# A recurrence and mixer kernel: first loads cast on the way, six masks on other engines, three sums ahead of the fourth

## The chip, the cores and the metric

One core of a Trainium2 chip. The metric is the device time of one execution in microseconds (us), and the smaller the better. Engines are named as in the profile: PE does matmuls and transposes, DVE, ACT and POOL work on elements, SP and POOL issue transfers. Unless a ratio is given, times are medians of runs of one kernel.

## The reference, cut to what matters

Four batches, eight heads, 768 steps of 64 elements. A decaying recurrence over q, k and v gives x; a token mixing and then a channel mixing follow.

```python
for t in range(S):                                    # per head, decay gamma
    state = gamma * state + outer(k[t], v[t])
    y[t]  = scale * q[t] @ state
x  = y as (batch, 768, 512)
u  = x + (relu(x^T @ w_tok1) @ w_tok2)^T              # token mixing, 768 -> 256 -> 768
out = u + relu(u @ w_ch1) @ w_ch2                     # channel mixing, 512 -> 1536 -> 512
```

The kernel does two heads (a "pair") at a time, in blocks of 128 steps. "ch1" and "ch2" are the two matmuls of the channel mixing. For batch 0 a half of ch1 is 12 groups of four matmuls, one for each pair, 48 in all. "All ch1" below means this first half.

## The kernel before

Every instruction is described as an `Op` with an engine, a priority, an assumed duration and what it depends on. A list scheduler, `arrange()`, then puts them into one order for each engine. So the order on PE is fixed when the kernel is built, by assumed times; on the chip PE follows it and waits where an input is late.

```python
        # front(b, p): loads of pair p of batch b, all through SP, all as float32
        for nm, src in (("k", k), ("q", q), ("v", v)):
            def emit(nm=nm, src=src):
                t = tile_of(sl[nm], sb, [P, 2 * NC, D], FP)
                ...
                    dma = nc.sync.dma_start(out=t, in_=rows.rearrange("h (c p) d -> p (h c) d", p=P))
                if b == 1:
                    tc.add_manual_dep(dma.ins, wops["c1", 1].ins.ins.name, ...,
                        reason="the weights come first")
        ...
        kc = op(KENG, 900, 980, emit, [ld["k"]], [K], [sl["k"]])       # k scaled, to f16, on DVE
        qc = op("POOL", 770, 830, cast(Q, sl["q"]), [ld["q"]], [Q], [sl["q"]])
        vc = op("POOL", 770, 830, cast(V, sl["v"]), [ld["v"]], [V], [sl["v"]])
        ...
        def turn(src, dst, dep, eng):        # six transposes on PE, then a copy out of PSUM
            ...
            t = op("PE", 340, 500, emit, [dep, ...], [T], [src])
        ...
        pp = op("PE", 300, 470, emit, [kc, vc, ...], [ST], [K, V])      # the first sum step, k^T v
        ...
                def emit(hf=hf, j=j, A=A):                              # the mask, 16 of them a batch
                    nc.vector.tensor_tensor(am, src[:, :HC], mask, ALU.mult)
        ...
        FA = "ba" if first else "fa"         # batch 0's token mixing: three PSUM buffers "ba"

    # back(b): the channel mixing
                for half_cts in (cts[:NP // 2], cts[NP // 2:]):
                    c1 = op("PE", 328, 490, lambda e=emit, q=half_cts: e(q),
                            [uT_done[b, p, sh] for p in range(NP)] + [wops["c1", ...], c1], ...)

    # at the end: zero matmuls ("fillers") where the schedule expects PE to wait at the start
                idle[0] = max(0, int((o.start - end - 40) / (220 if end > 1500 else 500)))
```

A "turn" is what the text calls the six transposes that bring k or q of a pair into the other layout.

Of the kernel before, what the change touches and what calls it, by code (L numbers as in the profile page):

```python
# [17 lines left out]
def kernel(  # L18
# [56 lines left out]
    make_identity(nc, ident16)  # L75

    gp = const_p.tile([P, NP], FP, name="gp")
    for p in range(NP):
# [4 lines left out]
    nc.gpsimd.affine_select(  # L83
        out=mask, in_=mask, compare_op=ALU.is_ge, fill=0.0,
        base=0, pattern=[[0, HC], [1, P]], channel_multiplier=-1,
    )
# [12 lines left out]
    BUFS = dict(kf=4, qf=4, vf=4, k16=3, q16=3, v16=4, kT=4, qT=4, U=3, am=8, x16=2, h1=4, u16=3, u16w=2,  # L99
# [3 lines left out]
    LONG, XK, XQ, XU, XBAR, RING = 2, 2, 2, 2, 1500, 3  # L103
# [18 lines left out]
    def arrange():  # L122


        way = {}
        for op in reversed(ops):
            if op.first is not None:
                way[op] = way.get(op, 0) + op.lat + SEM
                for d in op.deps:
                    way[d] = max(way.get(d, 0), way[op])  # L130
        for op in ops:
            if op.first is not None:
                op.prio = (op.prio[0], 0, EARLY * op.first - way[op], op.first)
        free = dict(PE=5000, ACT=5000, DVE=4600, POOL=4000, SP=1300, DMA=1300)
        taken = {t: [] for t in BUFS}
        todo, order, ring = list(ops), [], []
        while todo:
            best = []
            for op in todo:
                if any(d.end is None for d in op.deps):  # L140
                    continue
                start = free[op.eng]
                if op.dma and op.eng == "SP" and len(ring) >= RING:
                    start = max(start, ring[-RING])
                for d in op.deps:
                    if d.eng == op.eng and (d.dma or d.eng == "PE"):
                        continue
                    start = max(start, d.end + (30 if d.eng == op.eng else SEM) + op.guard)
                more = {}
                for s in op.takes:  # L150
                    q = taken[s.tag]
                    n = len(q) + more.get(s.tag, 0) - BUFS[s.tag]
                    more[s.tag] = more.get(s.tag, 0) + 1
                    if n >= 0:
                        old = q[n]
                        if any(u.end is None for u in old.users):
                            break
                        start = max([start] + [u.end + SEM for u in old.users])
                else:
                    best.append((start, op))  # L160
            t = min(b[0] for b in best)

            eng = min(best, key=lambda b: (b[0], b[1].prio))[1].eng
            start, op = min((b for b in best if b[1].eng == eng and b[0] <= t + 20),
                            key=lambda b: b[1].prio)
            free[op.eng] = start + op.occ
            op.start = start
            if op.dma:
                free["DMA"] = max(free["DMA"], start + 50) + op.dma
                op.end = free["DMA"] + 1600  # L170
                if op.eng == "SP":
                    ring.append(free["DMA"])
            else:
                op.end = start + op.lat
            for s in op.takes:
                taken[s.tag].append(s)
            todo.remove(op)
            order.append(op)
        return order
# [16 lines left out]
    def weight(key, ns, out, src, dep):  # L196
        def emit():
            return nc.gpsimd.dma_start(out=out, in_=src.rearrange("(i p) j -> p i j", p=P))
        wops[key] = Op("POOL", (0,) if key in ("t1", "t2", ("c1", 0)) else (1, 0, 99), 800, 800, emit, deps=[dep], dma=ns)


    load_done = [None]
# [4 lines left out]
    def front(b, p):  # L207
# [20 lines left out]
        sl, ld = {}, {}  # L228
        for nm, src in (("k", k), ("q", q), ("v", v)):
            sl[nm] = Slot(nm + "f")  # L230

            def emit(nm=nm, src=src):
                t = tile_of(sl[nm], sb, [P, 2 * NC, D], FP)
                rows = src[b, 2 * p:2 * p + 2]
                if nm == "q" and b < LONG:

                    dma = nc.sync.dma_start(  # L237
                        out=t.rearrange("p (h f i) d -> p h f (i d)", h=2, f=2),
                        in_=rows.rearrange("h (f p i) d -> p h f (i d)", f=2, p=P))
                else:  # L240
                    dma = nc.sync.dma_start(out=t, in_=rows.rearrange("h (c p) d -> p (h c) d", p=P))  # L241
                if b == 1:
# [4 lines left out]
            ld[nm] = Op("SP", (0, b, p), 100, 100, emit,  # L247
                        deps=[load_done[-1]] + ([wops["c1", 1]] if b == 1 else []),
                        takes=[sl[nm]], dma=1200 if nm == "q" and b < LONG else 1750)
            load_done.append(ld[nm])  # L250

        K, Q, V = Slot("k16"), Slot("q16"), Slot("v16")

        def emit():
            k16 = tile_of(K, sb, [P, NC, 2, D], F16)
            for j in range(2):
                h = 2 * p + j
                src = sl["k"].tile[:, j * NC:(j + 1) * NC, :]
                if KENG == "ACT":
                    nc.scalar.mul(k16[:, :, j, :], src, gk[:, h:h + 1])  # L260
                else:
                    nc.vector.tensor_scalar(k16[:, :, j, :], src, gk[:, h:h + 1], None, ALU.mult)  # L262
        KENG = "DVE"
        kc = op(KENG, 900, 980, emit, [ld["k"]], [K], [sl["k"]])

        def cast(slot, src):
            def emit():
                t = tile_of(slot, sb, [P, NC, 2, D], F16)
                nc.gpsimd.tensor_copy(t.rearrange("p c h d -> p h c d"),  # L269
                                      src.tile.rearrange("p (h c) d -> p h c d", h=2))  # L270
            return emit
        qc = op("POOL", 770, 830, cast(Q, sl["q"]), [ld["q"]], [Q], [sl["q"]])
        vc = op("POOL", 770, 830, cast(V, sl["v"]), [ld["v"]], [V], [sl["v"]])
        KT, QT = Slot("kT"), Slot("qT")

        def turn(src, dst, dep, eng):
            T = Slot("fa")

            def emit():
                T.tile = tp = tile_of(T, ps, [P, 512], FP).bitcast(F16)  # L280
                for c in range(NC):
                    nc.tensor.transpose(tp[:, c * P:(c + 1) * P],  # L282
                                        src.tile[:, c].rearrange("p h d -> p (h d)"), ident16)
# [11 lines left out]
        def crossbar(src, dst, dep):  # L295
            def emit():
# [3 lines left out]
                    in_=src.tile.rearrange("p c h d -> p (c h d)"))  # L300
# [7 lines left out]
        def emit():  # L308
            st = tile_of(ST, ps, [P, 512], FP)
            for c in range(NC - 1):  # L310
                for j in range(2):
                    nc.tensor.matmul(st[j * D:(j + 1) * D, c * D:(c + 1) * D], K.tile[:, c, j],  # L312
                                     V.tile[:, c, j], start=True, stop=True)
# [20 lines left out]
        def emit():  # L334
            nc.vector.tensor_scalar(RS.tile[D:, :, D:], US.tile[D:], g128[2 * p + 1], None, ALU.mult)
        r1 = op("DVE", 400, 480, emit, [prev, r0], [], [US, RS])
# [4 lines left out]
        for hf in range(2):  # L341
# [12 lines left out]
            for j in range(2):  # L354
                def emit(hf=hf, j=j, A=A):
                    am = tile_of(AM[2 * hf + j], sb, [P, HC, P], F16)
                    src = A[j].tile.rearrange("p (i t) -> p i t", t=P)
                    nc.vector.tensor_tensor(am, src[:, :HC], mask, ALU.mult)  # L358
                am_ops.append(op("DVE", 470, 550, emit, [a], [AM[2 * hf + j]], [A[j]]))
        X16 = Slot("x16")  # L360
        x_ops, xf = [], []
        for hf in range(2):
            Y = Slot("fa")

            def emit(hf=hf, Y=Y):
                y = tile_of(Y, ps, [P, 512], FP)
                R = RS.tile
                for i in range(HC):
# [5 lines left out]
                    for j in range(2):  # L374
                        nc.tensor.matmul(o[:, j * D:(j + 1) * D], AM[2 * hf + j].tile[:, i],  # L375
                                         V.tile[:, c, j], start=(c == 0), stop=(c == 0 or j == 1))
# [42 lines left out]
        FA = "ba" if first else "fa"  # L419
# [8 lines left out]
        t1 = op("PE", 690, 860, emit, x_ops + [wops["t1"], None if first else t2_done.get(b * NP + p - 1)], [T1], [X16])  # L428
# [10 lines left out]
        for hf in range(2):  # L439
# [9 lines left out]
            t2 = op("PE", 350, 520, emit, [hr, wops["t2"]], [T2], [H1])  # L449
# [64 lines left out]
    def back(b):  # L514
# [6 lines left out]
        for sh in range(2):  # L521
            H2 = Slot("h2")
            rel = []
            for ft in range(NF):
# [12 lines left out]
                for half_cts in (cts[:NP // 2], cts[NP // 2:]):  # L537
                    c1 = op("PE", 328, 490, lambda e=emit, q=half_cts: e(q),
                            [uT_done[b, p, sh] for p in range(NP)] + [wops["c1", int(ft >= CUT1[0][1])], c1],
# [8 lines left out]
            for i in range(HC):  # L548
# [3 lines left out]
                for part in range(parts):  # L552
# [25 lines left out]
                    op("SP", 100, 100, emit, [ad], [], [O]).dma = 800 // parts  # L578


    weight("t1", 2000, wt1, moe_w_tok1, None)
    weight("t2", 2000, wt2, moe_w_tok2, None)
    for i, (f0, f1) in enumerate(CUT1):
        weight(("c1", i), 650 * (f1 - f0), wc1[i], moe_w_ch1[:, f0 * P:f1 * P], None)
    weight(("c2", 0), 7800, wc2, moe_w_ch2, None)
    casts = [front(0, p) for p in range(NP)]
    after = {"t1": casts[2][2], ("c1", 0): casts[3][1]}
    last = None
    for key, o in wops.items():
        o.deps += [d for d in (after.get(key), last) if d is not None]  # L590
        last = o

    for b in range(1, B):
        for p in range(NP):
            front(b, p)
    for b in range(B):
        back(b)
    end, mixing = 1500, False
    for o in arrange():
        if o.eng == "PE":  # L600
            mixing = mixing or o.prio[0] == 1
            if o.takes and not mixing:

                idle[0] = max(0, int((o.start - end - 40) / (220 if end > 1500 else 500)))
# [32 lines left out]
```

## Time and profile before

| | before |
|---|---|
| time | 208.95 us (208.68 to 209.27, 3 runs) |
| span of the profiled run (208.47 us), clock | 206.8 us, 1.00 |
| last v of batch 0 landed, usable | 22.54 us, 24.40 us |
| first ch1 matmul | 37.91 us |
| batch 1's first k issued, landed | 34.56 us, 44.21 us |
| all ch1 and both turns of batch 1's first pair (counted) | 46.56 us |

The span runs from the first to the last instruction; the time is some 1.7 us longer. The clock is the mean share of full TensorE speed that the core was granted. The page gives PE's share and the two transfer queues; in the queue lines the numbers are packets, megabytes and a share of the 16 engines' span.

```profile
PE 198.9 (96%) x1898; PEld 120.5 (58%) x1898; DVE 114.8 (56%) x291; ACT 96.2 (47%) x205; POOL 61.9 (30%) x107
...
q1 hardware_dynamic: 89104, 29.89, 72.6%
q0 software_dynamic: 3664, 3.93, 11.4%
```

PE at 96% reads like a PE-bound kernel. It is one from 38 us on; before that its row holds fillers (62 records). A line of the timeline has the columns: start, us, engine, line, operation, output and inputs, shape, count, and in brackets the idle time before it and what ended it.

```profile
108.43 0.23 PE L372 MATMUL fa<-r,qT 128*128 128x128 f16 x1 [0.31 <-DVE r L335]
```

It is PE's only idle time over 0.1 us between 40 us and the tail.

### The profile page before, as it was taken

The numbers are of one execution on the slowest core, as the hardware profiler recorded it, in microseconds if no ns is written. First come the engines' busy times: TensorE is split into PE (matmuls) and PEld (weight loads), VectorE is DVE, ScalarE is ACT, GpSimd is POOL, SyncE is SP. The second block draws the span as 40 slices with busy tenths as digits, with TensorE's granted clock in tenths as the row PEclk, the third lists the DMA queues.
The fourth block names the chain that finished last, engine by engine and source line by source line (L and its number), as shares of the span: only waits on it lengthen the run. The fifth ranks groups of instructions, "written<-read, shape, count | busy, mean of one in ns | idle before, by whom it ended". The sixth has DMA issues, their size and how long they took to land.

```text
span 206.8 us, 4738 instructions
## 1 busy us (share of the span) xinstructions
PE 198.9 (96%) x1898; PEld 120.5 (58%) x1898; DVE 114.8 (56%) x291; ACT 96.2 (47%) x205; POOL 61.9 (30%) x107
## 2 busy tenths in 40 slices
PE   6899899999999999999999999999999999999993
PEld 2554487564667667576656574458556545545552
DVE  6377896114998878996794726686663021021021
ACT  7237458674497842455502670176215604604600
POOL 2338852113345635252533134115311000000000
PEclk9999999999999999999999999999999999999999
DMA  6999999999999999989995899996722012012012
GB/s 165 248 244 247 188 207 201 202 263 237 295 271 213 189 203 230 226 177 162 212 171 141 145 216 218 155 263 107 152 101 75 17 51 101 3 51 101 0 54 101
DMA packets 92790, 34.13 MB, mean 165 GB/s; under 512 B 81888, under 2 KB 89312, under 8 KB 92768
## 3 DMA queue, kind: packets, MB, share of 16 engines
q1 hardware_dynamic: 89104, 29.89, 72.6%
q0 software_dynamic: 3664, 3.93, 11.4%
q8 instruction: 15, 0.25, 0.5%
q14 instruction: 7, 0.06, 0.1%
HBM read 26.74 MB, written 6.29 MB: 160 GB/s over the span
## 4 chain that ended last, share of the span: by engine, by line
PE 83%; SPq 5%; DMA 4%; DVE 3%; ACT 2%; issue 1%; POOL 0%; DVEq 0%
PE ba L532 31%; PE ba L561 29%; PE fa L426 4%; DMA kf<-in_k_dram 4%; PE fa L447 4%; PE fa L351 3%; SPq L241 3%; PE fa L375 3%; SPq L237 2%; PE fa L372 2%; PE fa L282 2%; PE fa L312 2%; DVE k L262 1%; PE ba L426 1%; PE ba L189 1%
## 5 line engine op out<-in xcount | busy, mean ns | idle before, releaser
L532 PE MATMUL ba<-uT,wc 128*128 128x384 f16 x384 | 68.4, 326 | 0.0
L561 PE MATMUL ba<-wc,h 128*128 128x512 f16 (+1 forms) x300 | 67.7, 371 | 0.0
L545 ACT ACTIVATE h<-ba 128x384 f16<-128x384 f32 x96 | 46.7, 490 | 41.3 <-PE ba L532 40.4
L532 PEld LDWEIGHTS <-wc 128*128 128x128 f16 x384 | 35.5, 98 | 22.2
L570 DVE TENSOR_TENSOR o<-x,ba 128x512 f32<-128x512 f32 (+1 forms) x25 | 16.6, 663 | 50.1 <-PE ba L561 49.7
L561 PEld LDWEIGHTS <-h 128*128 128x128 f16 x300 | 27.6, 98 | 27.0
L358 DVE TENSOR_TENSOR am<-fa,mask 128x384 f16<-128x384 f32 x64 | 32.7, 550 | 5.3 <-PE fa L351 4.8
L403 POOL CAST x<-x 128x384 f16<-128x384 f32 x30 | 15.0, 512 | 37.6 <-issue 20.4
L269 POOL CAST q<-qf 128x768 f16<-128x768 f32 x16 | 13.7, 854 | 29.3 <-DMA qf<-in_q_dram 24.7
L386 ACT ACTIVATE x<-fa,gy 128x192 f32<-128x192 f32 (+1 forms) x42 | 15.1, 417 | 9.2 <-PE fa L375 8.7
L262 DVE TENSOR_SCALAR k<-kf,gk 128x384 f16<-128x384 f32 x32 | 14.5, 495 | 7.6 <-DMA kf<-in_k_dram 7.5
L189 PE MATMUL fa<-zero 128*128 128x512 f16 x54 | 15.9, 425 | 2.4 <-DVE zero L52 1.3
L331 ACT ACTIVATE r<-U 64x320 f16<-64x320 f32 x16 | 7.4, 465 | 23.2 <-DVE U L324 23.2
L324 DVE SCALAR_TENSOR_TENSOR U<-U,gp,fa 128x64 f32<-128x64 f32 x64 | 17.1, 275 | 1.0
L454 DVE TENSOR_TENSOR x<-x,fa 128x384 f32<-128x384 f32 x24 | 12.5, 549 | 6.3 <-POOL q L269 3.1
L291 ACT COPY qT<-fa 128x768 f16<-128x768 f16 x8 | 11.6, 1455 | 6.5 <-PE fa L282 6.5
L269 POOL CAST v<-vf 128x768 f16<-128x768 f32 x16 | 13.2, 827 | 4.6 <-DMA vf<-in_v_dram 3.7
L375 PE MATMUL fa<-v,am 128*128 128x64 f16 x192 | 13.9, 193 | 0.0
L375 PEld LDWEIGHTS <-am 128*128 128x128 f16 x192 | 12.1, 98 | 1.9
L426 PEld LDWEIGHTS <-wt 128*128 128x128 f16 x192 | 11.7, 98 | 2.6 <-issue 0.4
L447 PEld LDWEIGHTS <-wt 128*128 128x128 f16 x192 | 11.8, 98 | 2.0
L465 POOL CAST u16w<-x 128x384 f16<-128x384 f32 x16 | 7.9, 506 | 14.7 <-DVE x L454 14.6
(53 smaller groups left out, 164.3 us busy)
## 6 DMA issues: line engine op xcount, KB each, us to landing
kf<-in_k_dram SPq DMA_DIRECT2D x16, 384.0 KB, 6.5
qf<-in_q_dram SPq DMA_DIRECT2D x16, 384.0 KB, 6.1
vf<-in_v_dram SPq DMA_DIRECT2D x16, 384.0 KB, 5.8
out_dram<-o SPq DMA_DIRECT2D x23, 256.0 KB, 2.3
wc<-in_moe_w_ch_dram POOLq DMA_DIRECT2D x1, 1536.0 KB, 18.9
wc<-in_moe_w_ch_dram POOLq DMA_DIRECT2D x1, 1024.0 KB, 11.7
wt<-in_moe_w_tok_dram POOLq DMA_DIRECT2D x2, 384.0 KB, 6.9
wc<-in_moe_w_ch_dram POOLq DMA_DIRECT2D x1, 512.0 KB, 7.3
```

The costliest lines, as they stand in the source:

```text
L189: nc.tensor.matmul(slot.tile, zero[:, :P], zero, start=True, stop=True)
L262: nc.vector.tensor_scalar(k16[:, :, j, :], src, gk[:, h:h + 1], None, ALU.mult)
L269: nc.gpsimd.tensor_copy(t.rearrange("p c h d -> p h c d"), src.tile.rearrange("p (h c) d -> p h c d", h=2))
L324: nc.vector.scalar_tensor_tensor(U[:, c], U[:, c - 1], gp[:, p:p + 1], o, ALU.mult, ALU.add)
L358: nc.vector.tensor_tensor(am, src[:, :HC], mask, ALU.mult)
L375: nc.tensor.matmul(o[:, j * D:(j + 1) * D], AM[2 * hf + j].tile[:, i], V.tile[:, c, j], start=(c == 0), stop=(c == 0 or j == 1))
L426: nc.tensor.matmul(acc[:, jt * P:(jt + 1) * P], wt1[:, i, jt * P:(jt + 1) * P], X16.tile[:, i], start=(i == 0), stop=(i == NC - 1))
L447: nc.tensor.matmul(acc[:, i * P:(i + 1) * P], wt2[:, jt, t], H1.tile[:, jt], start=(jt == 0), stop=(jt == NJ - 1))
L532: nc.tensor.matmul(acc[:, :SH], w[:, ct, f * P:(f + 1) * P], UT.tile[:, ct, sh * SH:(sh + 1) * SH], start=(ct == 0), stop=(ct == NP - 1))
L545: nc.scalar.activation(H2.tile[:, ft], A.tile[:, :SH], AF.Relu)
L561: nc.tensor.matmul(A.tile[:, :CW], H2.tile[:, ft, i * P:(i + 1) * P], wc2[:, ft, cs], start=(ft == 0), stop=(ft == NF - 1))
L570: nc.vector.tensor_tensor(o[:, :CW], X.tile[:, sh * HC + i, cs], A.tile[:, :CW], ALU.add)
```

## The change

The intent: bring batch 0 in sooner and start ch1 sooner. q and v of batch 0 are cast to f16 by the transfer itself, which puts them on POOL's queue; k of pairs 1 to 3 goes there too. Six of batch 0's sixteen masks are made by an ACT copy and a POOL select. The ch1 sums of the first three pairs may go ahead of the fourth. The estimate behind the fillers is cut by a quarter. The diff also moves the token mixing of pairs 2 and 3 from the three buffers "ba" to the five called "fa". The core of it:

```diff
-    LONG, XK, XQ, XU, XBAR, RING = 2, 2, 2, 2, 1500, 3
+    RING = dict(SP=3, POOL=8)
+    ASIDE, RACT = ((1, 1), (1, 3), (2, 1), (2, 3), (3, 1), (3, 3)), ()
+    FILL, TOKBA = 0.75, 2
 ...
+                eng = nc.gpsimd if first and p else nc.sync
 ...
+        def cast(slot, nm):
+            if first:
+                def emit():
+                    t = tile_of(slot, sb, [P, 2 * NC, D], F16)
+                    ...
+                    return nc.gpsimd.dma_start(out=t, in_=rows.rearrange("h (c p) d -> p (h c) d", p=P))
+                o = Op("POOL", (0,), 1000, 1000, emit, [], [slot], dma=QLONG if nm == "q" else 1400)
+                queue.append(o)
+                return o
 ...
+                    if src is Q and first:
+                        for j in range(2):
+                            nc.tensor.transpose(tp[j * D:(j + 1) * D, c * P:(c + 1) * P],
+                                                src.tile[:, j * NC + c], ident16)
+                        continue
 ...
+                    if off:
+                        nc.scalar.copy(am, src[:, :HC])
+                    else:
+                        nc.vector.tensor_tensor(am, src[:, :HC], mask, ALU.mult)
+                if off:
+                    def emit(M=M):
+                        nc.gpsimd.affine_select(out=M.tile, in_=M.tile, compare_op=ALU.is_ge, ...)
 ...
-        FA = "ba" if first else "fa"
+        FA = "ba" if first and p < TOKBA else "fa"
 ...
-                for half_cts in (cts[:NP // 2], cts[NP // 2:]):
-                    c1 = op("PE", 328, 490, lambda e=emit, q=half_cts: e(q),
-                            [uT_done[b, p, sh] for p in range(NP)] + ...
+                for some in (cts[:NP - 1], cts[NP - 1:]):
+                    c1 = op("PE", 164 * len(some), 164 * len(some) + 160, lambda e=emit, q=some: e(q),
+                            [uT_done[b, p, sh] for p in some] + ...
 ...
-                idle[0] = max(0, int((o.start - end - 40) / (220 if end > 1500 else 500)))
+                idle[0] = max(0, int((o.start - end - 40) * FILL / 220 if end > 1500 else (o.start - end) / 450))
```

(Cut: the scheduler's new model of two queues, the order of POOL's issues, the identity and the mask made later.)

## The prediction

> **What bounds the kernel now.** I read the page's forty slices first, then the sums by stretch, the chain that ended last, the timeline of the first 56 us, and the trace's landing and packet records behind it.
>
> The slices show two regimes.
>
> ```profile
> PE   6899899999999999999999999999999999999993
> DVE  6377896114998878996794726686663021021021
> PEclk9999999999999999999999999999999999999999
> DMA  6999999999999999989995899996722012012012
> ```
>
> A slice is 5.17 us. PE looks busy from the second slice on, but until about 38 us part of that is filler: L189 multiplies zeros and holds 15.9 us. DMA is at 9 from the second slice to the nineteenth. The stretches and the chain say when PE becomes the true bound:
>
> ```profile
> 20.00:25.00 5.00, 4.21 (x46) 1.91 (x42) 4.05 (x13) 3.02 (x6) 3.72 (x5) 1.00 1.29 198
> 25.00:30.00 5.00, 4.95 (x92) 4.24 (x89) 4.60 (x13) 2.62 (x8) 2.82 (x6) 1.00 1.16 198
> ...
> 60.00:80.00 20.00, 20.00 (x263) 14.14 (x262) 16.90 (x40) 12.44 (x28) 9.84 (x17) 1.00 1.14 209
> 80.00:120.00 40.00, 39.69 (x443) 25.27 (x442) 30.56 (x76) 17.42 (x41) 14.50 (x26) 1.00 1.02 180
> 120.00:160.00 40.00, 40.00 (x381) 24.07 (x378) 23.31 (x52) 14.99 (x36) 12.81 (x22) 1.00 0.86 160
> ```
>
> ```profile
> 12.24 7.61 DMA kf<-in_k_dram
> ...
> 38.08 7.80 PE ba L532 x48
> ```
>
> The columns of the first are stretch, length, then busy us of PE, PEld, DVE, ACT, POOL, clock, DMA share, GB/s. From 38 us PE has some 0.3 us of idle time until the tail. So the 168.8 us from there to the end (206.8 - 38.0) are PE work in one row, and this change leaves that work alone. Only two things can move the time: when the first ch1 matmul starts, and whether PE waits after that.
>
> The first 38 us are paced by DMA. By the landing records the twelve loads of batch 0 land from 4.52 us (first k) to 22.54 us (last v), each k or v about 1.75 us behind the one before it, each q about 1.25. Then, without a gap, land wt1 24.65, wt2 26.52, the first ch1 weights 29.30, the rest of ch1 34.49, ch2 43.27. Batch 1's loads may only be issued when the ch1 weights are in, and run beside ch2's:
>
> ```profile
> 34.56 0.37 SPq L241 DMA_DIRECT2D kf<-in_k_dram  x1
> ...
> 37.91 7.96 PE L532 MATMUL ba<-uT,wc 128*128 128x384 f16 x48
> ...
> 44.23 0.75 DVE L262 TENSOR_SCALAR k<-kf,gk 128x384 f16<-128x384 f32 x2 [7.20 <-DMA kf<-in_k_dram]
> ...
> 45.53 0.83 POOL L269 CAST q<-qf 128x768 f16<-128x768 f32 x1 [7.86 <-DMA qf<-in_q_dram]
> ...
> 46.15 0.50 PE L282 MATMUL fa<-ident,k 128*128 128x128 f16 x6
> ```
>
> The reader is to see that batch 1's first k was issued at 34.56 and landed only at 44.21, after ch2. DVE and POOL sat idle for it, PE did not: its first use of that k, the turn at 46.15, stands behind all 48 ch1 matmuls. That slack is 1.2 us.
>
> **What the Trainium skill says.** "DMA: Bandwidth & Descriptors", section "SWDGE vs HWDGE vs iDMA": a DMA that casts must be issued from GpSimd. The trace agrees as far as it goes: the weights, the only casting loads, are on q0, software_dynamic, 3664 packets. Its section "Issuing engines are not separate DMA queues" says that all issuers share the same 16 DMA engines; so a second queue adds no bandwidth, and I count bytes and packets, not queues. Its section "Queues, rings and completion order" says that each engine goes round-robin between its queues by packet. The packet records agree: from 39 to 41 us, q0 (ch2) started 155 and 150 packets in the two microseconds and q1 (k) 148 and 159, though a ch2 packet reads eight times the bytes; and kf's first packets came only at 38.0, 3.5 us after the issue. "TensorE: Matmul & The Clock Gate", Part 1, says that an idle window of about 3.4 us drops the clock; the trace has no such gap and a clock of 1.00 everywhere.
>
> **The change, part by part.**
>
> *Cast loads for batch 0.* q and v come as f16 through POOL's queue; k of pairs 1 to 3 joins them; only the first k is left on SP. Removed: eight POOL casts of 0.83 us (6.6 us of POOL), which stood between a landing and its use. The last v is usable at its landing instead of 24.40 (cast start 23.56 + 0.84). Added: eleven issues on POOL. The weights' issues took 0.70 to 1.03 us each, so about 10 us, done well ahead of the data. What a casting packet costs I fit on the weights' landings: wt1, 48 packets per engine of 1024 B source, 2.11 us, 44 ns each; the second ch1 piece, 32 of 4096 B, 5.19 us, 162 ns. A line through both is 4.7 ns + 0.0384 ns per byte (wt2's 3072 B: 122 against 117 measured). Estimates from it: v, 96 packets of 256 B, 14.5 ns each, 1.4 us; q, 32 of 768 B, 34 ns, 1.1 us. With k at 1.75 a pair costs 4.25 us, four 17.0. From the first packets at 2.0 us, with 0.5 us to land, that is 19.5 for the last v; I take 20.0, because k through the software queue was never seen and the small packets are extrapolated. So inputs and every weight behind them come about **2.5 us** earlier.
>
> *Six masks by ACT and POOL.* Six of sixteen DVE masks at 0.55 us go: 3.3 us off DVE, which is 4.6 of 5 busy from 25 to 30 us. Each becomes an ACT copy (about 0.47) and a POOL select (0.52 for the same size, L83 at start), longer in latency but beside other work. Worth perhaps 0.5 to 1 us in the last pair's chain.
>
> *First ch1 sums.* The ordering of instructions shows what it comes to: three ch1 matmuls, one group's three pairs, ahead of the last transpose. 3 x 0.163 = 0.5 us.
>
> *Fillers.* L189's issues go from about 60 to 40; they stand in waits, and the removal gains at most tenths where one overran. The q turn has twelve half-width matmuls instead of six: 4 x 0.34 = 1.3 us of PE at worst, while PE waits anyway.
>
> Sum up to the first ch1 matmul: before, 13.5 us from usable v (24.40) to 37.91. After, 20.0 + about 13 = **33 us**, some 5 us earlier, if nothing else binds.
>
> **But most of this should be lost again.** The new PE order puts batch 1's k turn after 35 of the 48 ch1 matmuls, not behind all 48, and PE is in order. PE would reach it at 33 + 35 x 0.163 = 38.7. That k still has to wait for the ch1 weights and to share with ch2; both move by only the 2.5 us: landing 44.2 - 2.5 = 41.7, scaled by DVE (0.75 and a start) at 42.5. PE idles almost 4 us. Then turn 0.34, 12 ch1 1.96, q turn 0.34, last ch1 0.16: at 45.3 all ch1 and both turns are done. Before, the same work (ch1 done 45.88, plus two turns of 0.34) counts to 46.56. Gain **1.25 us**, or in general the DMA's gain less 1.25. Later turns have slack: the second k lands near 46.2 and is wanted near 51. From there PE is the bound again.
>
> **Rivals.**
> 1. *The start binds, not the load*: if batch 1's k comes in time, the whole gain at the first ch1 stays, 4 to 5 us, 204 to 205 us. For: POOL and DVE are relieved, and someone chose this order. Against: kf's 9.65 us from issue to landing beside ch2, which the change does not touch.
> 2. *Small casting packets are dear*: their recorded durations extrapolate to 34 ns for v's 256 B against 24 for k's on SP. If throughput followed that, a pair would cost 1 us or more extra, and inputs come 3 us later: 212 to 214 us. Against: packets overlap, and landings fit the line above.
> 3. *POOL becomes the bound*: issues, six selects and sixteen casts stand in one in-order row, and the first x cast is caught between weight issues. It could cost 1 to 2 us at the start; as the wait for k has almost 4 us of room, little of it would show: 207 to 209 us.
> 4. *The clock drops in the 4 us wait*: then some us of matmuls run slow, up to 2 us lost, 209 to 210 us. It would need a whole quiet window.
>
> **Range and chances.** The middle case is 208.95 - 1.25 = 207.7; I lean slightly to the fast side for rival 1 and for k packets that may be cheaper in the software queue (if like v's, three times 0.35 us): 207.3 us. An input gain of 0.5 to 4 us gives 209.7 to 206.2; with some room for rival 1, 205.0 to 209.3. Faster by over 2% (under 204.8) needs rival 1 nearly in full: 0.16. Slower by over 2% (over 213.1) needs rival 2 in full: 0.03.
>
> **What would show it.** Right: last v landing near 20 and ch2 near 41; first ch1 matmul between 32 and 35 us; PE idle for 3 to 4 us before the k turn of batch 1, released by DVE, itself released by kf; from about 46 us on, PE's row as before. Wrong: no such idle time (rival 1); last v landing after 22 (rival 2); the first ch1 matmul after 37 with POOL as releaser (rival 3); a clock below 1.00 (rival 4); or new idle time of PE after 60 us, which I have counted as nil.

## The result, and the profile after

206.81 us (205.84 to 207.07, 4 runs) against 209.08 us of before in the same session: ratio 0.9893, 95% interval 0.9857 to 0.9929. A ratio here is the mean time of one kernel's fast runs over the mean of the other's in the same rounds, so not quite the ratio of the medians quoted. The profiled run took 205.84 us, span 204.1 us, clock 1.00.

| | before | predicted | after |
|---|---|---|---|
| last v landed | 22.54 | 20.0 | 19.70 |
| ch2's weights landed | 43.27 | 41 | 40.75 |
| first ch1 matmul | 37.91 | 33 | 33.66 |
| batch 1's first k landed | 44.21 | 41.7 | 41.66 |
| PE idle before that k's turn | 0 | almost 4 | 2.81 |
| all ch1 and both turns | 46.56 | 45.3 | 45.45 |
| last ch2 matmul issued | 202.95 | | 200.63 |

The slices of the changed kernel (5.10 us each), and the lines that answer to those of before on the page:

```profile
PE   6598999769999999999999999999999999999993
...
DMA  7999999989799999999997999898531112012012
...
q1 hardware_dynamic: 76128, 25.57, 61.3%
q0 software_dynamic: 12320, 6.69, 23.2%
```

PE's ninth slice, 40.8 to 45.9 us, is a 6, where the two slices ahead of it are 9 and 7. Batch 0's inputs have moved from q1 to q0. Sums by stretch make the hole sharper (length; busy us of PE, PEld, DVE, ACT, POOL; clock; DMA share; GB/s):

```profile
40.00:42.00 2.00, 0.00 (x0) 0.00 (x0) 0.32 (x1) 0.00 (x0) 0.00 (x0) 1.00 1.10 232
42.00:44.00 2.00, 1.51 (x14) 1.06 (x15) 0.43 (x2) 0.96 (x2) 0.83 (x1) 1.00 0.96 214
```

From 40 to 42 us PE does nothing at all, and the transfer engines are as busy as ever. The timeline says what it waits for:

```profile
31.45 0.38 SPq L256 DMA_DIRECT2D kf<-in_k_dram  x1
...
33.66 0.65 PE L597 MATMUL ba<-uT,wc 128*128 128x384 f16 x3
...
34.31 5.36 PE L597 MATMUL ba<-uT,wc 128*128 128x384 f16 x32
...
41.68 0.75 DVE L313 TENSOR_SCALAR k<-kf,gk 128x384 f16<-128x384 f32 x2 [8.46 <-DMA kf<-in_k_dram]
...
42.49 0.51 PE L332 MATMUL fa<-ident,k 128*128 128x128 f16 x6 [2.81 <-DVE k L313]
...
42.84 2.11 PE L597 MATMUL ba<-uT,wc 128*128 128x384 f16 x12
```

The reader is to see the order on PE: 35 ch1 matmuls, then the turn of batch 1's k, then the last 13. The turn stands where the schedule expected k to be in. It came at 41.66 us, DVE scaled it in 0.75 us, and 13 matmuls that had all they needed stood behind it.

Where the 2.63 us between the two profiled spans lie: 1.1 us up to 45 us (the table's sixth row); 0.3 us after the last ch2 matmul; and 1.2 us in between, which I had counted as nil. Start-to-start times of PE's instructions give most of that 1.2: the idle 0.31 us at 108.43 is gone, and 0.8 us lie in the ch1 matmuls. They step at 0.16 us, but 0.26 us where one of the matmuls of half the rows or columns (the scores, the sum step) follows; after 45 us there are 12 such steps before and 4 after. Nobody put them there: the schedule fell out otherwise.

### The profile page after: what moved, and what is told of

The parts are those of the page before. It is cut to its first block, busy times and chain, and to the rows that moved or that the text cites. A ratio compares the mean times of both kernels' runs of the same rounds, so it can differ in the third digit from the quotient of the medians.

```text
span 204.1 us, 4737 instructions
## 1 busy us (share of the span) xinstructions
PE 192.3 (94%) x1900; PEld 118.8 (58%) x1900; DVE 112.6 (55%) x285; ACT 97.4 (48%) x211; POOL 69.2 (34%) x116
## 4 chain that ended last, share of the span: by engine, by line
PE 81%; DMA 8%; DVE 6%; ACT 2%; issue 1%; POOL 0%; POOLq 0%; DVEq 0%
PE ba L626 31%; PE ba L597 28%; DMA kf<-in_k_dram 5%; PE fa L491 5%; PE fa L512 4%; PE fa L403 4%; DMA v<-in_v_dram 3%; PE fa L440 2%; DVE k L313 2%; PE fa L437 2%; PE fa L361 2%; DVE am L416 1%; PE fa L332 1%; ACT qT L340 1%; DVE U L373 1%
## 5 line engine op out<-in xcount | busy, mean ns | idle before, releaser
L626 PE MATMUL ba<-wc,h 128*128 128x512 f16 (+1 forms) x300 | 68.9, 371 | 0.0
L610 ACT ACTIVATE h<-ba 128x384 f16<-128x384 f32 x96 | 46.4, 492 | 39.2 <-PE ba L597 38.7
L597 PEld LDWEIGHTS <-wc 128*128 128x128 f16 x384 | 36.0, 98 | 22.5
L416 DVE TENSOR_TENSOR am<-fa,mask 128x384 f16<-128x384 f32 x58 | 29.9, 551 | 11.8 <-PE fa L403 11.7
L519 DVE TENSOR_TENSOR x<-x,fa 128x384 f32<-128x384 f32 x28 | 14.5, 551 | 11.6 <-PE fa L512 11.2
L313 DVE TENSOR_SCALAR k<-kf,gk 128x384 f16<-128x384 f32 x32 | 15.8, 534 | 8.5 <-DMA kf<-in_k_dram 8.5
L292 POOL CAST q<-qf 128x768 f16<-128x768 f32 x12 | 10.2, 849 | 21.4 <-DMA qf<-in_q_dram 20.5
L292 POOL CAST v<-vf 128x768 f16<-128x768 f32 x12 | 9.9, 827 | 8.6 <-DMA vf<-in_v_dram 7.9
L194 PE MATMUL fa<-zero 128*128 128x512 f16 x37 | 10.7, 423 | 2.2 <-DVE zero L52 1.3
L340 ACT COPY qT<-fa 128x768 f16<-128x768 f16 x8 | 11.5, 1443 | 2.1 <-PE fa L328 1.7
```

The costliest lines, as they stand in the source:

```text
L292: nc.gpsimd.tensor_copy(t, src.tile.rearrange("p (h c) d -> p h c d", h=2))
L313: (nc.gpsimd if keng == "POOL" else nc.vector).tensor_scalar(k16[:, :, j, :], src, gk[:, h:h + 1], None, ALU.mult)
L597: nc.tensor.matmul(acc[:, :SH], w[:, ct, f * P:(f + 1) * P], UT.tile[:, ct, sh * SH:(sh + 1) * SH], start=(ct == 0), stop=(ct == NP - 1))
L610: nc.scalar.activation(H2.tile[:, ft], A.tile[:, :SH], AF.Relu)
L626: nc.tensor.matmul(A.tile[:, :CW], H2.tile[:, ft, i * P:(i + 1) * P], wc2[:, ft, cs], start=(ft == 0), stop=(ft == NF - 1))
```

## The experiments

Twelve kernels. The runs of one batch share their runs of the kernel before: 208.65 us for the first four, 209.0 for the next four, 208.86 for the last four. Theory: PE's place for batch 1's first turn is what throws away the earlier start, because the k behind it is tied to the weights. Rivals: the six masks or the fillers are what counts; the clock falls in the wait; or the loads alone do it.

| run | what it is | time, us | ratio to before (95%) |
|---|---|---|---|
| e1 | both turns held behind ch2's first matmuls | 203.49 | 0.9748 (0.9730 to 0.9767) |
| e2 | 12 fillers in the wait | 205.76 | 0.9877 (0.9846 to 0.9908) |
| e3 | batch 1's first k ahead of ch2's weights | 203.92 | 0.9768 (0.9748 to 0.9788) |
| e4 | masks on DVE | 207.81 | 0.9948 (0.9917 to 0.9979) |
| e5 | the changed kernel again | 207.15 | 0.9900 (0.9865 to 0.9934) |
| e6 | loads of batch 0 as before | 213.96 | 1.0241 (1.0210 to 1.0272) |
| e7 | the cast loads alone | 208.95 | 0.9996 (0.9975 to 1.0017) |
| e8 | ch1 in halves, after all four pairs | 207.06 | 0.9917 (0.9879 to 0.9954) |
| e9 | e1, and the first sum step held | 205.32 | 0.9845 (0.9815 to 0.9875) |
| e10 | e9 with masks on DVE | 203.71 | 0.9753 (0.9735 to 0.9771) |
| e11 | e9 with loads of batch 0 as before | 208.16 | 0.9970 (0.9953 to 0.9986) |
| e12 | e9 with all token mixing in "ba" | 204.68 | 0.9798 (0.9780 to 0.9815) |

### e1: the turns held back

```diff
             t = op("PE", 340, 500, emit, [dep, ...], [T], [src])
+            if (b, p) == (1, 0):
+                late.append(t)
 ...
     for b in range(B):
         back(b)
+    late[0].deps.append(ch2[1])      # k turn not before the 4th ch2 matmul
+    late[1].deps.append(ch2[4])      # q turn not before the 10th
```

> The changed kernel with one ordering rule added: batch 1's first k turn not before the fourth ch2 matmul, its q turn not before the tenth. No DMA is touched. My theory (the new order puts the k turn 2.8 us before its data): the idle 2.81 us of PE before the k turn goes, k still lands near 41.7 us, ch2's weights near 40.7; span 204.1 - 2.8 = 201.3, time about 203 to 204, ratio to before 0.971 to 0.976, clock 1.00 in all runs. Rival (DMA bounds that stretch whatever the order): the wait only moves to ch2's weights, v or the second pair, and the time stays at 206 to 207.

203.49 us. The timeline:

```profile
33.30 7.48 PE L600 MATMUL ba<-uT,wc 128*128 128x384 f16 x45
...
40.62 1.03 PE L629 MATMUL ba<-wc,h 128*128 128x512 f16 x4
40.81 0.75 DVE L314 TENSOR_SCALAR k<-kf,gk 128x384 f16<-128x384 f32 x2 [8.60 <-DMA kf<-in_k_dram]
...
41.62 0.51 PE L333 MATMUL fa<-ident,k 128*128 128x128 f16 x6
...
44.79 0.35 PE L364 MATMUL fa<-v,k 128*64 128x64 f16 x10 [0.60 <-POOL v L293]
```

The 45 last ch1 matmuls run in one piece, ch2's first four fill the time until k is there, and the turn has no bracket: nothing waited. Some 3 us come from rules that only change an order. What is left is 0.60 us at the sum step, which waits for the cast of v. (ch2 starts 4.7 us earlier than in the profile after, 0.7 of it because the turns come later; of the 4.0 left, 2.5 remain at the last ch2 matmul. The later part came out 1.5 us longer in this order.)

### e2: fillers in the wait

```diff
                 T.tile = tp = tile_of(T, ps, [P, 512], FP).bitcast(F16)
+                if (b, p) == (1, 0) and src is K:
+                    idle[0] = 12
```

> The changed kernel with twelve zero matmuls (2.6 us) put into the wait before batch 1's first k turn; everything else is the same, so PE is busy in the 2.8 us in which it idles now. Theory of the clock (of the changed kernel's runs, four show 0.992 and a span of 205.1 to 205.7, one 1.00 and 204.1; the wait trips the clock in those): all runs at clock 1.00 and near the fastest, 205.8, median 1 us below the changed kernel's. Rival (the 0.992 has another cause): still mixed, median 206.8.

This keeps PE multiplying zeros through the wait, 38.49 to 41.24 us, with 0.71 us idle left. Four of six runs are at 205.3 to 206.1 us, two at 207.1; one of these is at clock 0.992, the other at 1.00. So "all runs at clock 1.00" failed. The 0.992 is rarer here, one of six against nine of eleven of the changed kernel (counted at e5), and not gone; and something else of about 1.5 us is in one run, which no trace shows.

### e3: the other remedy, k ahead of ch2's weights

```diff
-                eng = nc.gpsimd if first and p else nc.sync
+                eng = nc.gpsimd if (first and p) or (b, p, nm) == (1, 0, "k") else nc.sync
 ...
-                if b == 1:
+                if b == 1 and (p, nm) != (0, "k"):       # this k no longer waits for the ch1 weights
 ...
+            elif (b, p, nm) == (1, 0, "k"):
+                o = Op("POOL", (0,), 1000, 1000, emit, [], [slot], dma=ns)
+                queue.insert(queue.index(wops["c2", 0]), o)
```

(The places of the turns, the sum step and the scores on PE are held as in the changed kernel.)

> The changed kernel with batch 1's first k loaded through POOL's queue, ahead of ch2's weights, and the first two turns, score and sum steps of batch 1 held to the places that they have now. Theory (the wait at the k turn is the load's place behind ch2): k lands near 33 us in place of 41.7, no PE idle time before the k turn, which stands at about 40; ch2 lands about as now or 1 us later (41 to 42) and is wanted at about 42.8; time 203 to 204.5. Rival (total DMA volume bounds): the wait reappears before the first ch2 matmul or the q turn, and the time stays above 206.

k landed at 32.67 instead of 41.66 us, and with the order on PE unchanged the wait is gone:

```profile
34.53 5.36 PE L607 MATMUL ba<-uT,wc 128*128 128x384 f16 x32
39.73 0.50 PE L336 MATMUL fa<-ident,k 128*128 128x128 f16 x6
40.07 2.11 PE L607 MATMUL ba<-uT,wc 128*128 128x384 f16 x12
```

203.92 us. So the transfer and the place are two ends of one thing; by the ratios moving either one is worth some 3 us (0.9893 and 0.9900 to 0.9768 here, to 0.9748 in e1). What was overtaken pays: ch2's weights land only at 42.99, a microsecond later than I had expected, and the first ch2 matmul follows at 43.04. (The edit moves q too: no longer behind that k, it landed at 39.78 instead of 42.83.)

### e4: the masks back on DVE

```diff
-    ASIDE, RACT = ((1, 1), (1, 3), (2, 1), (2, 3), (3, 1), (3, 3)), ()
+    ASIDE, RACT = (), ()
```

> The changed kernel with all sixteen masks of batch 0 on DVE again. Prediction's theory (six masks off DVE are worth 0.5 to 1 us up to the first ch1 matmul, but the wait for batch 1's k hides it): first ch1 matmul at 34.5 to 35.3 in place of 33.7 to 34.3, the k still landing near 41.7, PE's idle time before it shorter by as much, time unchanged within 0.5 us. Rival (the masks matter to the time): 1 us or more slower.

207.81 us, so my "within 0.5" failed and the rival's figure held. But the run changes two things: the scheduler now puts the k turn after 31 of 48 ch1 matmuls, which leaves 17 instead of 13 behind it. Nor did the start come later, as I had expected: the first ch1 matmul was at 33.01 us and the fourth at 34.32 (33.66 and 34.31 in the profile after). The k was in at 40.97, and three of the six runs had a clock of 0.990 or less. I take no worth of the masks from it; e10 was made for that.

### e5: the changed kernel again

No edit to what runs on the chip.

> The changed kernel, unaltered, for its spread on one chip beside the next three, and in the hope of a profile with a clock of 0.992 (four of five of its runs had it, with a span 1.0 to 1.6 us longer). If the 0.992 comes of the wait for batch 1's k, the clock record shows half speed from about 42 us for 3.4 us; if it comes of the start or of the idle tail, it stands there. Median 206.8, ratio to before 0.989.

207.15 us, as expected. Its profiled execution shows what the profile after did not:

```profile
42.13 0.82 PE L332 MATMUL fa<-ident,k 128*128 128x128 f16 x6 [3.47 <-DVE k L313]
...
42.75 3.38 PE L597 MATMUL ba<-uT,wc 128*128 128x384 f16 x12
```

```profile
42.00:44.00 2.00, 1.87 (x10) 1.23 (x11) 0.08 (x1) 1.01 (x2) 0.83 (x1) 0.50 1.02 215
44.00:46.00 2.00, 2.00 (x10) 1.04 (x9) 0.00 (x0) 1.00 (x3) 0.83 (x1) 0.67 0.95 233
```

The same 12 matmuls take 3.38 us instead of 2.11, and the clock column reads 0.50. The trace's clock record has half speed from 41.90 us for 3.413 us. Start to start, turn and 12 matmuls took 3.83 us against 2.29: the clock costs 1.5 us here. It can also be counted from the times: of the changed kernel's eleven executions in the two sessions (five with the result, six here), two had clock 1.00 (205.84 and 205.62 us) and nine had 0.992 (206.80 to 207.96, mean 207.2).

### e6 and e7: the rest without the cast loads, the cast loads without the rest

```diff
 e6
-                eng = nc.gpsimd if first and p else nc.sync
+                eng = nc.sync                      # and q, v cast by POOL, q's turn full width, as before
 e7
-    ASIDE, RACT = ((1, 1), ...), ()
-    FILL, TOKBA = 0.75, 2
+    ASIDE, RACT = (), ()
+    FILL, TOKBA = 1.0, 4                           # and ch1 in halves, after all four pairs
```

> The changed kernel with batch 0's loads as before: float32 through SP's queue, casts on POOL; masks, ch1 order and fillers as changed. Prediction's theory (the inputs' DMA time and the casts behind it are the gain, and it passes to the time less what the k turn takes): the last v lands at 22.5 again, batch 1's k at 44.2, the first ch1 matmul no earlier than 36; time 208.5 to 210 (its k turn stands even earlier in the order, after 27 of 48 ch1 matmuls, so it waits for k and has more left after it). Rival (the masks, the ch1 order or the fillers carry the gain): below 207.5.

> The cast loads alone: masks all on DVE, ch1 in halves that wait for all four pairs, the old filler rule, the old PSUM buffers for the token mixing. Theory (time is set by batch 1's k, which only DMA moves): last v near 19.7, k near 41.7 as in the changed kernel; the k turn stands after 22 of 48 ch1 matmuls, so 26 are left behind it against 13, which are 13 x 0.163 = 2.1 us more after the wait; with two score steps there too (0.44) that earlier stood later: 208 to 209. Rival (each part adds its own share): 207.5 or less.

e6 took 213.96 us, four more than I expected at most. The last v landed at 22.82, the first ch1 matmul was at 35.40, and the k turn stood after 27 matmuls:

```profile
45.73 0.76 PE L333 MATMUL fa<-ident,k 128*128 128x128 f16 x6 [4.86 <-DVE k L310]
46.29 3.58 PE L598 MATMUL ba<-uT,wc 128*128 128x384 f16 x12
```

The wait is 4.86 us and half speed comes with its end. The clock record has it for 3.413 us again, as it has in e8 after a wait of 3.51. All six runs of e6 had a clock of 0.992 or less, three of them 0.984 or less, which is what two such windows would give (half of 2 x 3.413 us in 212 us is 0.016).

e7 took 208.95 us: as expected, nothing gained. What I had not expected is why. The last v was in at 20.12 us, and yet ch1 started only at 36.47, 1.4 us earlier than before:

```profile
35.83 0.34 PE L543 MATMUL ba<-ident,u 128*128 128x128 f16 x3
36.00 0.38 PE L194 MATMUL ba<-zero 128*128 128x512 f16 x1
36.29 0.34 PE L543 MATMUL ba<-ident,u 128*128 128x128 f16 x3
36.47 1.79 PE L597 MATMUL ba<-uT,wc 128*128 128x384 f16 x10
```

The last transposes come one by one with fillers between them, all in "ba". But the loads are not without effect on the start. Against the fourth ch1 matmul of the kernel before (38.40 us), the cast loads alone come 1.4 us earlier (36.96), the rest alone 2.0 (36.40, e6), and both together 4.1 (34.31 in the profile after): each brings a part. Neither part alone brought any time; PE then waited at the k turn, 1.85 us in e7 and 4.86 in e6.

### e8: ch1 in halves, as before

```diff
-                for some in (cts[:NP - 1], cts[NP - 1:]):
+                for some in (cts[:NP // 2], cts[NP // 2:]):      # each waiting for all four pairs
```

> The changed kernel with ch1 in two halves that wait for all four pairs. The k turn then stands after 30 of 48 ch1 matmuls in place of 35. Theory: the first ch1 matmul is 0.5 us later, which the wait for k hides; but five matmuls (0.8 us) more stand behind the wait: 0.3 to 0.9 us slower than the changed kernel of the same rounds. Rival (the three early ch1 matmuls bring what the prediction gave them and no more): 0.5 us slower at most, and then whatever the k turn's place.

207.06 us, ratio 0.9917 against 0.9900 of e5 in the same batch. The intervals overlap, so the 0.3 to 0.9 us that I expected it to be slower did not show, and the k turn moved again (after 30 matmuls). One of its six executions is at 0.992, the profiled one (209.19 us, the slowest). The worth of the three early sums stays within the noise.

### e9 to e12: the parts, without the wait that hides them

With the turns held, the last four runs try the parts where their worth should show. e9 is e1 and one more rule, against e1's last 0.60 us:

```diff
+        if (b, p) == (1, 0):
+            late.append(pp)
 ...
+    late[2].deps.append(ch2[7])      # the first sum step not before the 16th ch2 matmul
```

> The run with both turns of batch 1's first pair moved behind the first ch2 matmuls, and in addition the first sum step of that pair moved behind the sixteenth ch2 matmul. My theory (PE waits for whatever of batch 1 is placed ahead of its load's landing, and only the place is at fault): the 0.60 us idle gap at 44.8 us is gone, no gap of PE over 0.2 us between 34 and 60 us, span near 201.0, time 202.9, ratio to the kernel before 0.971 to 0.973. Rival (the work behind the sum step, that is the masks and the x of batch 1, is then late for its own users): a new gap of 0.5 us or more appears later, between 48 and 60 us, and the time stays at 203.5 or more.

The 0.60 us are gone, and the kernel is slower than e1: 205.32 us. Its timeline has one new gap over 0.2 us, far from where either theory looked:

```profile
84.41 0.22 PE L445 MATMUL fa<-v,am 128*128 128x64 f16 x2
85.58 0.23 PE L442 MATMUL fa<-r,qT 128*128 128x128 f16 x1 [0.95 <-DVE r L392]
```

DVE's row has an addition of the token mixing (84.47, 0.55 us) between the state's last step and this r. The rule moved one instruction at 45 us; the list scheduler then chose otherwise 40 us later. In the profile e9 ends 1.94 us after e1 at the last ch2 matmul: 1.05 at the first ch2 matmul, where PE's order is still the same in both, so a later start (last v landed at 20.21 against 19.52), and 0.9 after it. Two of its six executions also had the clock at 0.992, without a wait of PE like that of the changed kernel in its trace; where, stays open.

The other three are each e9 with one thing put back: `ASIDE` empty, as in e4 (e10); batch 0's loads as before, as in e6 (e11); and

```diff
-    FILL, TOKBA = 0.75, 2
+    FILL, TOKBA = 0.75, 4            # e12
```

> The run of the turns and the first sum step held back, with the six masks back on DVE. The places of batch 1's first instructions are now the same in both, behind all of ch1, so the masks are seen without the wait that hid them. My theory (masks off DVE are worth 0.5 to 1 us in the last pair's chain): fourth ch1 matmul 0.5 to 1 us later than in the run with the masks aside, time 0.4 to 1.0 us longer, 203.3 to 203.9. Rival (the last pair's chain is set by the landing of v and by PE, not by DVE): fourth ch1 matmul and time within 0.3 us of the run with the masks aside.

> The run of the turns and the first sum step held back, with batch 0's loads as float32 through SP and the casts on POOL, as in the kernel before. My theory (the loads' worth is the earlier last v and everything behind it, and shows in full once PE does not wait for batch 1): last v at 22.8 us, fourth ch1 matmul near 36.4 us against 33.3 to 34.3, batch 1's k at 44.9 us and read no sooner than 45; time 3 us longer than with the cast loads, 205.5 to 207, still 2 to 3 us below the kernel before. The run of plain loads without the held turns took 213.96; if the held turns remove its wait and its half-speed clock, this one is 7 us or so shorter. Rival (plain loads are slow for another reason than the wait, such as POOL's casts holding up the later pairs): it stays above 210.

> The run of the turns and the first sum step held back, with the token mixing of all four pairs of batch 0 in the three PSUM buffers called ba, as in the kernel before; the change moved that of the last two pairs to the five called fa, and my prediction passed over this. If these buffers are part of why ch1 starts early (the run with the cast loads alone, mixing in ba, had its first ch1 matmul only at 36.5 us): fourth ch1 matmul 1 to 2 us later than with fa, time 1 to 2 us longer, 204 to 205. If they are not: both within 0.3 us.

| | e9 | e10 masks on DVE | e11 plain loads | e12 mixing in ba |
|---|---|---|---|---|
| last v landed | 20.21 | 19.54 | 22.75 | 20.03 |
| fourth ch1 matmul | 34.35 | 34.39 | 36.59 | 35.38 |
| first ch2 matmul | 41.66 | 42.12 | 44.78 | 42.69 |
| first to last ch2 matmul | 158.4 | 156.2 | 158.2 | 156.7 |
| time | 205.32 | 203.71 | 208.16 | 204.68 |

At the first ch2 matmul every one of them is later than e9, and two of them are faster in the end, because e9's later part is the worst of the four. So for the masks and the buffers the whole time says nothing about the part that was changed, and only the start can be read.

*Buffers (e12).* From 18 us until 30.1 us the two kernels run alike to within 0.1 us (up to 0.6 apart before, while loads were landing). Then:

```profile
31.54 0.83 PE L517 MATMUL fa<-h,wt 128*128 128x128 f16 x12
32.56 1.30 PE L548 MATMUL fa<-ident,u 128*128 128x128 f16 x9 [0.19 <-POOL u L535]
33.70 0.65 PE L602 MATMUL ba<-uT,wc 128*128 128x384 f16 x3
```

is e9, and

```profile
32.00 0.38 PE L194 MATMUL ba<-zero 128*128 128x512 f16 x1 [0.21 <-DVE x L524]
32.21 0.33 PE L548 MATMUL ba<-ident,u 128*128 128x128 f16 x3
32.38 0.83 PE L517 MATMUL ba<-h,wt 128*128 128x128 f16 x12
33.11 0.33 PE L548 MATMUL ba<-ident,u 128*128 128x128 f16 x3
```

is e12: the second mixing step comes later and the transposes are strung out. The fourth ch1 matmul is 1.03 us later, and so is the first ch2. The 1 to 2 us expected of the start held; the longer time did not.

*Masks (e10).* The fourth ch1 matmul is level, where I had expected 0.5 to 1 us, but with inputs that landed 0.67 us earlier; the first ch2 is 0.46 us later. If the start follows the landing, the masks are worth some 0.7 us at the fourth ch1 and 1.1 us at the first ch2. That is an estimate from one execution each; the same program's start has moved by 1.0 us between two executions (33.66 and 32.64 us in the profile after and in e5). The time went the other way.

*Loads (e11).* Against e9 the fourth ch1 matmul is 2.2 us later, the first ch2 3.1 and the time 2.8: here alone start and time agree, with each other and with the 3 us expected, and it is the best measure of the cast loads that the runs give. Against e6 it is 208.16 us for 213.96: the wait before the first k turn is down to 0.62 us, and no run fell below clock 0.997. It missed my 205.5 to 207, with 0.31 us more at ch2's weights and 0.48 us at the next pair's turn. With plain loads there is still next to nothing won over the kernel before (0.997).

The best version is e1, level with e10 within their intervals: 203.49 us, 2.5% under the kernel before and, by the two ratios, some 1.5% under the changed kernel.

## Why the prediction was right, and where it was lucky

**The start.** Right. The last v was in at 19.70 against 20.0 predicted and ch1 began at 33.66 against 33. The terms behind it were less good. Once running, a pair took 3.7 to 3.9 us instead of 4.25: k 1.55 to 1.75 and v 1.35 to 1.45, much as estimated, but q 0.7 to 0.8 instead of 1.1 us, a mis-sized term. The first pair ate that up: its v landed at 8.22 us, where the same sum gives 6.75.

**The loss at the k turn.** Right. The wait was 2.81 us in one execution and 3.47 in another, against "almost 4": PE got there a microsecond later than worked out (39.7 against 38.7), while k came as expected (41.66, predicted 41.7). All ch1 and both turns were done at 45.45, predicted 45.3; the gain up to there 1.1 against 1.25. e1 and e3 show the cause from both ends: take away the place or the lateness of k, and some 3 us more are gained. About 1 us of that is the clock (rival 4), not the wait: no run of e1 or e3 fell below 0.997, and against the two executions of the changed kernel at 1.00 (205.84 and 205.62 us) e1 is 2.2 us faster and e3 1.8.

**Rival 1** (k comes in time) did not happen, but e3 is that case made on purpose, and it took 203.92 us; I had put it at 204 to 205. **Rivals 2 and 3** did not happen.

**Rival 4** (the clock falls in the wait) did happen. Nine of eleven executions show the clock at 0.992, and e5's, the one of them with a kept trace, has the drop at the wait. I had given it too little room. The Trainium skill's "TensorE: Matmul & The Clock Gate", Part 1, puts the clock at half after an idle window of about 3.4 us, with windows that run free of the kernel. The trace agrees on the length: half speed for 3.413 us in e5, which cost 1.5 us. But the prediction's "a whole quiet window" was wrong. The recorded stretches of clock end on a grid of 3.413 us, so they show where the windows lie. In the window just ahead of a drop PE was busy 0.11 us (e6), 0.18 (e5) and 0.83 (e8); windows with 1.44 us (profile after), 1.55 (e7) and 1.66 (e4) were followed by none. The 2.81 us of the profile after were spread over two windows, 1.97 and 0.84 us; that fits, with PE's busy time in the window as what decides, but no run was made to test it.

**After 46 us** "PE's row as before" was wrong. The later part ran 1.2 us faster, because the schedule came out with fewer costly steps and without one gap, and the tail 0.3, for which I have no cause. Together this was worth more than the part I had worked out. It and the clock were both left out of the middle case, and they pull against each other: 1.1 + 1.2 + 0.3 is 2.6 us between the two profiled executions, both at clock 1.00, and the clock takes 1.5 back in most others. Between the medians 2.3 us were measured, also because the profiled execution of the kernel before (208.47 us) lies 0.6 under its median (209.08). So the mechanism up to 46 us was right; that the number was near is in part luck, two omissions of opposite sign.

**Fillers.** Records of them fell from 62 to 40 (18.5 to 11.5 us). "At most tenths" is doubtful: in the kernel before, the chain that ended last runs through 1.9 us of fillers between 24 and 36 us behind which the next matmul shows no wait (0.59 at 24.21, 0.54 at 25.07, 0.43 at 31.58, 0.33 at 35.25), in the profile after through 0.75 us (at 24.84). This is an upper bound, and no run isolates it.

**Small readings.** The prediction's 15.9 us of fillers are those written to "fa" alone. Its 168.8 us of PE work hold 3.5 us of tail: PE's last matmul ended at 203.2. Of batch 0's last pair, k landed 2.5 us and v 1.4 us behind the load before it, not about 1.75. None of these changes the sums behind the range.

**What I passed over.** I put the earlier start down to loads and masks and did not mention the PSUM buffers at all; e12 shows 1.0 us of the start there. And I called the cast loads worth what they land earlier, less the k turn; e7 shows them worth nothing in time alone, and e11 against e9 some 2.8 us once the turns are held.

**What stays open.** The worth of the masks and of the three early sums to better than 0.5 us, since every edit reorders the later part by as much; that of the fillers, of q's half-width transposes and of the scheduler's new model, none of which a run changes alone; the slow run of e2 at full clock; the place of the half-speed window in two runs of e9.

## What to carry to other kernels

Where the order of an in-order engine is fixed at build time, look at the first instruction that needs a transfer of the next stage, and ask whether ready work stands behind it: holding it a few matmuls later was worth more here than the whole change. A wait of PE can cost twice: here waits of 3.5 and 4.9 us were also followed by 3.4 us at half speed. And where a scheduler lays out everything anew on each edit, judge a part by the stage it acts on, not by the total: later accidents of 1 to 2 us are as large as what is being measured.

## What the Trainium skill lacked or had wrong

- "DMA: Bandwidth & Descriptors", section "Queues, rings and completion order", gives the turn-taking by packet but not what it does to a transfer that comes second: batch 1's k was issued at 31.45 us and its first packets came at 35.0, 3.5 us later; it landed after 10.2 us where the same 384 KB took 1.75 us in steady flow at the start.
- The same page, section "SWDGE vs HWDGE vs iDMA", has a packet of at most 4096 B by preference. The trace agrees for the k loads on POOL's queue (4096-B packets of sixteen 256-B rows, 232 to 274 ns each in the mean of a load, so 14 to 17 ns a row), but the page does not say that the same load on SP's queue goes as 256-B packets (18 to 26 ns), nor that casting loads are not gathered (128 B and 384 B written per packet, 32 to 34 and 51 to 61 ns). In steady flow k took about 1.75 us per load on either queue.
- "TensorE: Matmul & The Clock Gate", Part 1, agrees on the window (3.413 us), but does not say how idle an idle window is: 0.83 us of PE work in it did not keep the clock up (e8), 1.44 us did (profile after).
- "TensorEngine Tiling", section "Key Properties", says that changing the tiling mode drains the engine, without a size. A matmul of 64 rows or columns after a full one stepped 0.10 us later than a full one would (0.26 against 0.16 us after ch1); whether it is that drain, no run here isolates.
